# Full contraction rows for the key-value tails, an earlier root for the second half of batch 0, and another order for batch 1's and 2's casts

## The chip, the cores and the metric

The kernel runs on one core of a Trainium2 chip. The metric is the device time of one execution in microseconds (us); lower is better. The kernel before has a median of 335.21 us over three runs (334.85 to 335.27). On the core, TensorE (PE) does the matrix products, VectorE (DVE), ScalarE (ACT) and GpSimd (POOL) the elementwise work and the casts, and SyncE (SP) issues nearly all transfers. PEld is PE's weight load.

## The reference

A linear attention with a normalisation for each head, then a gated feed-forward network (FFN):

```python
# q, k, v: [8, 8, 576, 64] (batch, head, position, head_dim)
kv = np.einsum('bhsd,bhse->bhde', k, v)
out = np.einsum('bhsd,bhde->bhse', q, kv)
rms = np.sqrt(np.mean(out * out, axis=-1, keepdims=True) + 1e-06)
out = out / rms * g_norm
x = out.transpose(0, 2, 1, 3).reshape(8 * 576, 512)
# FFN: w_gate, w_val [512, 1536], w_out [1536, 512]
rms = np.sqrt(np.mean(x * x, axis=-1, keepdims=True) + 1e-06)
xn = x / rms * rms_g
g = xn @ w_gate
result = (g / (1 + np.exp(-g)) * (xn @ w_val)) @ w_out    # [4608, 512], float32
```

## The kernel before, in words

**Tiling.** The 576 positions of a batch are 512 main rows (four tiles of 128) and 64 tail rows. The FFN runs in nine stages of 512 rows: one for the main rows of each batch (n = 0 to 7) and one for the tail rows of all eight (n = 8). A stage has twelve steps `up(j)`: four products with the gate weights into the PSUM tile g_ps, four with the value weights into v_ps, then SiLU on ACT and the multiplication h_sb on DVE. Four steps `down(c)` follow, of twelve products each with w_out into o_ps; ACT copies the result and SP stores it. A step is eight products of 128x512, a `down` twelve.

**Attention.** For each batch, `kv_pair` (L259) multiplies keys and values of two heads into a 128x128 state: for batches 0 and 1 from a packed layout (L264), for batches 2 to 7 (L272) with four products of 128 rows and a fifth of the 64 tail rows, which stand in tile `t == T` of the buffers. There are two key and two value buffers, kbs and vbs, used in turn by even and odd batches. The states go to kv_all (L303, L304). Then come q times state (`o`), squares and sums, an inverse root (`head`, `guess`, `root`), the scaled rows xna (`scale`) and their turn into the layout xnt that the FFN reads.

**Order.** Each engine does its instructions in the order in which the code emits them, and semaphores hold them until their inputs are there. So the order in the code is the schedule. From stage n = 1 on, the lists `steps[u]` hold the work that is emitted behind step u: the attention of the next batch, and casts and loads of the batch after that.

**The start.** Batch 0 is done in two halves of 256 columns: A, then Z. Its root is ACT's Sqrt (L441) and DVE's reciprocal (L444), both in `root_by_table`; then ACT loads its table for SiLU (L718). Weights come in blocks of columns (`load_w`), and `round_w` (L196) casts and scales them to bf16. Block 1 covers steps 2 and 3, block 2 steps 4 to 7, block 3 steps 8 to 11. Half A's columns are used by `up_pair(i, 0)`, half Z's by `up_pair(i, 256)`; between them xna of Z is turned on PE (`x_turn`, L634) and DVE copies it to xnt.

**Between stage 0 and stage 1.** Stage 0's `down` is cut in pieces (`down_part`), and batch 1's attention stands between them: key-value products, the turns of q (L770), the columns `f_cols` and their squares, the sums, F.head and F.root on DVE, F.scale (xna, L448), and `f_x`, which turns xna on PE (L280) and copies it to xnt on ACT or DVE. The PSUM pool att_ps has two banks, so a third tile waits until the first has been read. `round_wo` casts the out weights wo_sb, three blocks of four tiles, `cast_kv` and `cast_q` the keys, values and queries (both through L106 on ACT and L108 on the other engines).

**Loads.** All large loads go through SP in order into a ring of seven staging buffers (`st`); a load waits until the casts of its buffer's old content are done.

Of the kernel before, what the change touches and what calls it, by code (L numbers as in the profile page):

```python
# [20 lines left out]
def kernel(  # L21
# [20 lines left out]
    T = 4  # L42
# [216 lines left out]
    def kv_pair(ps, b, j, first, last):  # L259
        if b < EARLY:  # L260
            for c in range(C):
                for u in range(2):
                    rows = slice(u * D, u * D + D)
                    PE.matmul(  # L264
                        ps[rows, rows], lhsT=pairs_buf(b, "k")[rows, j, c, :], rhs=pairs_buf(b, "v")[rows, j, c, :],
                        start=(first and c == 0), stop=(last and c == C - 1),
                    )
            return
        hs = slice(2 * j, 2 * j + 2)
        for t in range(T + 1):  # L270
            n = TAIL if t == T else 128
            PE.matmul(  # L272
                ps, lhsT=bufs[b]["k"][0:n, t, hs, :], rhs=bufs[b]["v"][0:n, t, hs, :],
                start=(first and t == 0), stop=(last and t == T),
            )

# [430 lines left out]
    for s in range(NS):  # L707
        round_w(1, "g", s, SC)
        round_w(1, "v", s, GP)
# [7 lines left out]
    Z.root_by_table(lambda: None)  # L717
# [3 lines left out]
    xs = [Z.scale(c, oZ[c]) for c in range(2)]  # L721
    halves = [ffn.up_pair(0, 0)]
    ffn.gate_pair(0, 0, halves[0])
    nothing = lambda: None
    turnsZ = (nothing, lambda: x_turn(Z, 0, xs[0], DVE), lambda: x_turn(Z, 1, xs[1], DVE))
    halves.append(ffn.up_pair(1, 0, turnsZ))
# [31 lines left out]
    A1 = None  # L758
# [74 lines left out]
    round_wo_halves(2)  # L833
# [58 lines left out]
    for n in range(1, B + 1):  # L892
# [6 lines left out]
        if n == 1:  # L899
            for i in KV_CASTS:  # L900
                steps[i // 2 % 2] += [lambda i=i: cast_kv(2, "v", i, GP if i == NS else SC if i % 2 else DVE)]
        if n < B:
            a = atts[n + 1]
            late = n == 1
            if not a.tail:
                steps[late] += [lambda a=a: a.kv_products((0, 1))]
                steps[1 + late] += [lambda a=a: a.kv_products((2, 3)), a.kv_copy]
            for c in range(T):
                u = (3, 5, 6, 8)[c] if late else 2 + 2 * c
# [58 lines left out]
```

## Time and profile before

| | |
|---|---|
| median of 3 runs | 335.21 us (334.85 to 335.27) |
| profiled execution | 334.25 us |
| its span on the core | 332.4 us |
| granted TensorE clock | 0.999 |
| loaded and stored | 37.75 MB read, 9.44 MB written |
| stage n = 1 starts (first g_ps of L467) | 59.70 us into the span |

The span is the time from the first to the last instruction that the profiler saw; the execution's time has 1.85 us around it. Times in the rows of a timeline are microseconds from the span's start: start, length, engine, line, operation, output<-inputs, shapes and count, and in brackets the idle time ahead of it with what ended it. Rows of groups give the summed busy time in us and the mean of one in ns. In the table of stretches, the columns are the stretch, its length, the busy time of PE, PEld, DVE, ACT and POOL with counts, the granted PE clock, the busy share of the DMA engines and GB/s.

### The profile page before, as it was taken

The numbers are of one execution on the slowest core, as the hardware profiler recorded it, in microseconds if no ns is written. First come the engines' busy times: TensorE is split into PE (matmuls) and PEld (weight loads), VectorE is DVE, ScalarE is ACT, GpSimd is POOL, SyncE is SP. The second block draws the span as 40 slices with busy tenths as digits, with TensorE's granted clock in tenths as the row PEclk, the third lists the DMA queues.
The fourth block names the chain that finished last, engine by engine and source line by source line (L and its number), as shares of the span: only waits on it lengthen the run. The fifth ranks groups of instructions, "written<-read, shape, count | busy, mean of one in ns | idle before, by whom it ended". The sixth has DMA issues, their size and how long they took to land.

```text
span 332.4 us, 5037 instructions
## 1 busy us (share of the span) xinstructions
PE 318.9 (96%) x1876; PEld 156.5 (47%) x1908; DVE 181.3 (55%) x367; ACT 179.6 (54%) x316; POOL 18.2 (5%) x37
## 2 busy tenths in 40 slices
PE   6889997999999999999999999999999999999994
PEld 3665454554444444444454445444544444444441
DVE  4865658359616771578057905791478156813410
ACT  3577655555765575556655665667465255223321
POOL 1232206100000000000000000000000000000000
PEclk9999999999999999999999999999999999999999
DMA  8999999585279626971697079966300630060014
GB/s 265 346 381 387 374 370 250 179 281 145 47 144 299 177 33 154 299 182 21 153 298 193 16 144 195 297 146 156 95 2 0 153 102 0 3 173 17 0 34 96
DMA packets 73861, 54.87 MB, mean 165 GB/s; under 512 B 42088, under 2 KB 65644, under 8 KB 73836
## 3 DMA queue, kind: packets, MB, share of 16 engines
q1 hardware_dynamic: 73536, 53.95, 58.0%
q10 hardware_dynamic: 300, 0.59, 0.5%
q8 instruction: 15, 0.25, 0.3%
q14 instruction: 10, 0.08, 0.1%
HBM read 37.75 MB, written 9.44 MB: 142 GB/s over the span
## 4 chain that ended last, share of the span: by engine, by line
PE 84%; DMA 5%; DVE 5%; ACT 2%; issue 1%; SPq 1%; DVEq 0%
PE v_ps L467 26%; PE g_ps L467 26%; PE o_ps L504 23%; PE att_ps L272 3%; DMA st<-in_moe_w_gate_dram 3%; DMA st<-in_q_dram 2%; PE att_ps L338 2%; DVE xna L448 1%; SPq L380 1%; DVE xna L373 1%; DMA xnt<-xna 1%; PE v_ps L504 1%; DVE h_sb L473 1%; PE g_ps L484 1%; PE v_ps L484 1%
## 5 line engine op out<-in xcount | busy, mean ns | idle before, releaser
L473 DVE TENSOR_TENSOR h_sb<-silu,v_ps 128x512 bf16<-128x512 bf16 x104 | 71.1, 684 | 113.2 <-PE v_ps L467 71.9
L467 PE MATMUL v_ps<-xnt,wv_sb 128*128 128x512 bf16 x412 | 106.1, 379 | 0.4
L467 PE MATMUL g_ps<-xnt,wg_sb 128*128 128x512 bf16 x399 | 104.5, 379 | 1.2 <-issue 0.5
L472 ACT ACTIVATE silu<-g_ps 128x512 bf16<-128x512 f32 x104 | 62.5, 601 | 68.3 <-PE g_ps L467 62.8
L504 PE MATMUL o_ps<-wo_sb,h_sb 128*128 128x512 bf16 x398 | 89.4, 379 | 0.7 <-issue 0.2
L504 PEld LDWEIGHTS <-h_sb 128*128 128x128 bf16 x432 | 41.2, 98 | 49.8 <-DVE h_sb L473 2.4
L467 PEld LDWEIGHTS <-wv_sb 128*128 128x128 bf16 x416 | 40.7, 98 | 49.1
L467 PEld LDWEIGHTS <-wg_sb 128*128 128x128 bf16 x416 | 38.2, 98 | 41.3 <-issue 1.1
L106 ACT COPY o_sb<-o_ps 128x512 f32<-128x512 f32 x34 | 19.9, 586 | 39.4 <-PE o_ps L504 36.5
L356 DVE TENSOR_REDUCE ssq<-sq 128x16 f32<-128x1024 bf16 x28 | 34.1, 1220 | 1.0
L347 ACT ACTIVATE sq<-att_ps 128x512 bf16<-128x512 f32 x28 | 16.7, 597 | 14.2 <-PE att_ps L338 11.3
L106 ACT CAST vb<-st 128x512 bf16<-128x512 f32 (+2 forms) x35 | 20.5, 630 | 4.8 <-DMA st<-in_v_dram 4.8
L373 DVE TENSOR_TENSOR xna<-outa,s1y 128x512 bf16<-128x512 bf16 x28 | 17.5, 685 | 0.2
L349 ACT CAST outa<-att_ps 128x512 bf16<-128x512 f32 x28 | 16.2, 580 | 0.0
L106 ACT CAST kb<-st 128x512 bf16<-128x512 f32 (+1 forms) x25 | 14.0, 619 | 0.0
L106 ACT CAST qb<-st 128x1024 bf16<-128x1024 f32 (+1 forms) x13 | 12.5, 1009 | 1.0 <-DMA st<-in_q_dram 1.0
L272 PE MATMUL att_ps<-vb,kb 128*128 128x128 bf16 (+1 forms) x120 | 12.4, 222 | 0.0
L355 DVE TENSOR_TENSOR sq<-sq,gsq 128x512 bf16<-128x512 bf16 x28 | 11.7, 418 | 0.0
L272 PEld LDWEIGHTS <-kb 128*128 128x128 bf16 (+1 forms) x120 | 8.6, 97 | 6.1
L338 PEld LDWEIGHTS <-qt 128*128 128x128 bf16 x96 | 7.4, 98 | 5.7
L338 PE MATMUL att_ps<-kv_all,qt 128*128 128x128 bf16 x96 | 9.3, 219 | 0.0
L579 PE MATMUL att_ps<-kv_all 128*128 128x256 bf16 (+1 forms) x34 | 7.5, 352 | 1.2 <-DVE sel L568 1.2
(122 smaller groups left out, 158.5 us busy)
## 6 DMA issues: line engine op xcount, KB each, us to landing
out_dram<-o_sb SPq DMA_DIRECT2D x16, 512.0 KB, 3.1
st<-in_q_dram SPq DMA_DIRECT2D x7, 1024.0 KB, 6.4
st<-in_k_dram SPq DMA_DIRECT2D x6, 1024.0 KB, 9.6
st<-in_v_dram SPq DMA_DIRECT2D x6, 1024.0 KB, 10.9
st<-in_moe_w_out_dram SPq DMA_DIRECT2D x3, 1024.0 KB, 14.8
st<-in_moe_w_gate_dram SPq DMA_DIRECT2D x2, 1024.0 KB, 12.3
st<-in_moe_w_val_dram SPq DMA_DIRECT2D x2, 1024.0 KB, 13.1
st<-in_k_dram SPq DMA_DIRECT2D x4, 288.0 KB, 5.0
```

Source lines behind the costliest of these rows:

```text
L106: engine.copy(out=dst, in_=src)
L272: PE.matmul(ps, lhsT=bufs[b]["k"][0:n, t, hs, :], rhs=bufs[b]["v"][0:n, t, hs, :], start=(first and t == 0), stop=(last and t == T),)
L338: PE.matmul(cols, lhsT=self.qt[:, j, 128 * c : 128 * c + 128], rhs=kv_all[:, self.n, j, :], start=(j == 0), stop=(j == NS - 1),)
L347: SC.activation(out=self.sq[c][:, 0], in_=ps, func=ACT.Square)
L349: SC.copy(out=self.outa[c], in_=ps)
L355: DVE.tensor_tensor(out=sq[:, 1], in0=sq[:, 0], in1=gsq8, op=OP.mult)
L356: DVE.reduce_sum(out=self.ssq[:, c], in_=sq, axis=AX.X)
L373: DVE.tensor_tensor(out=self.xna[c], in0=self.outa[c], in1=self.alpha[:, c, :].to_broadcast([128, H, D]), op=OP.mult)
L467: PE.matmul(ps, lhsT=wt[:, s, j * 128 : (j + 1) * 128], rhs=x[:, s, :], start=(s == 0), stop=(s == NS - 1),)
L472: SC.activation(out=silu, in_=g_ps, func=ACT.Silu)
L473: DVE.tensor_tensor(out=self.h[:, j, :], in0=silu, in1=v_ps, op=OP.mult)
L504: PE.matmul(self.o_ps[c], lhsT=self.h[:, j, c * 128 : (c + 1) * 128], rhs=wo_sb[:, j, :], start=(j == 0), stop=(j == NF - 1),)
```

## The change

The tail product of batches 2 to 7 takes all 128 rows of its tile. The upper 64 rows of the tail tile are set to zero once in each of the four buffers, on POOL (`clear_tail_rows`): in the even pair after half Z has been scaled, in the odd pair after batch 1's products. In the start, Z's root is emitted ahead of the casts of weight block 1, which are shared out over ACT, DVE and POOL; the turns of Z follow the gate products of step pair 1 instead of standing among its value products. For batch 1, v's load moves behind the first out weights, casts of k, v, q, of the out weights and of value weight block 3 change their engines and places, and key-value products and q turns move one `down_part` later. Batch 2's q and k casts leave POOL for ACT and DVE. In stage 1, the key-value products of batch 2 and its first `o` move one step later. From stage 1 on, `guess` is emitted behind step 11 instead of step 10.

```diff
         for t in range(T + 1):
-            n = TAIL if t == T else 128
             PE.matmul(
-                ps, lhsT=bufs[b]["k"][0:n, t, hs, :], rhs=bufs[b]["v"][0:n, t, hs, :],
+                ps, lhsT=bufs[b]["k"][:, t, hs, :], rhs=bufs[b]["v"][:, t, hs, :],
...
+    def clear_tail_rows(i, engine):
+        for t in (kbs[i], vbs[i]):
+            engine.memset(t[TAIL:128, T], 0.0)
...
-    for s in range(NS):
-        round_w(1, "g", s, SC)
-        round_w(1, "v", s, GP)
...
-    Z.root_by_table(lambda: None)
+    Z.root_by_table(lambda: round_w(1, "g", 2, DVE))
+    round_w(1, "g", 0, SC)
+    round_w(1, "g", 3, SC)
+    round_w(1, "g", 1, GP)
     SC.preload_act_table(ACT.Silu)
 
     ffn = Ffn(0)
     xs = [Z.scale(c, oZ[c]) for c in range(2)]
+    for s in range(NS):
+        round_w(1, "v", s, GP if s < 2 else DVE)
+    clear_tail_rows(0, GP)
     halves = [ffn.up_pair(0, 0)]
+    def turnsZ():
+        x_turn(Z, 0, xs[0], DVE)
+        x_turn(Z, 1, xs[1], DVE)
+    halves.append(ffn.up_pair(1, 0, (lambda: None, turnsZ)))
     ffn.gate_pair(0, 0, halves[0])
...
-    for name in ("k", "v"):
-        alloc_kv(1, name)
-        load_kv(1, name, nc.sync)
+    alloc_kv(1, "k")
+    load_kv(1, "k", nc.sync)
     load_wo(0)
+    alloc_kv(1, "v")
+    load_kv(1, "v", nc.sync)
     load_q(1)
...
-    for s in range(NS):
+    for s in (2, 3):
         round_w(3, "v", s, GP)
     for j in range(4, NF):
         ffn.up(j)
         for s in {4: (0, 1), 5: (2,), 6: (3,)}.get(j, ()):
             round_w(3, "g", s, SC)
-        if 5 <= j < 9:
-            cast_kv(1, "k", j - 5, DVE)
+        if j == 6:
+            for s in (0, 1):
+                round_w(3, "v", s, DVE)
         if j >= 8:
-            cast_kv(1, "v", j - 8, SC)
-        if j == 10:
-            round_wo(0, 0, 1, DVE)
-    for i in range(1, 4):
-        round_wo(0, i, 1, GP)
+            cast_kv(1, "k", j - 8, DVE)
+        if j == 7:
+            for i in range(4):
+                round_wo(0, i, 1, GP)
+    for i in range(NS):
+        cast_kv(1, "v", i, DVE if i % 2 else SC)
     for i in range(4):
-        cast_q(1, slice(2 * i, 2 * i + 2), DVE)
+        cast_q(1, slice(2 * i, 2 * i + 2), SC if i == 2 else DVE)
...
-    for c in range(4):
-        down_part(c, 0, 4)
-        if c == 0:
-            att1.kv_products((0, 1, 2, 3))
-            att1.kv_copy()
-        if c in (1, 2):
-            turns.q_turn(c - 1, SC if c == 1 else DVE)
-    round_wo_halves(1)
+    down_part(0, 0, 4)
+    down_part(1, 0, 4)
+    att1.kv_products((0, 1, 2, 3))
+    att1.kv_copy()
+    down_part(2, 0, 4)
+    turns.q_turn(0, SC)
+    turns.q_turn(1, DVE)
+    down_part(3, 0, 4)
+    round_wo(1, 0, 2, DVE)
+    for i in (2, 3):
+        round_wo(1, i, 1, GP)
+    for i in range(4):
+        round_wo(2, i, 1, GP)
+    clear_tail_rows(1, GP)
...
-    round_wo_halves(2)
...
-    f_x(0, xs[0], DVE)
+    f_x(0, xs[0], SC)
     f_x(1, xs[1], SC)
     ffn.down_out(1)
+    alloc_q(2)
+    cast_q(2, slice(0, 4), SC)
     down_part(2, 8, 12)
     f_x(2, xs[2], DVE)
-    f_x(3, xs[3], SC)
+    f_x(3, xs[3], DVE)
...
+    cast_q(2, slice(4, 8), DVE)
...
-    alloc_q(2)
-    for i in range(4):
-        cast_q(2, slice(2 * i, 2 * i + 2), GP)
-    for i in KV_CASTS:
-        cast_kv(2, "k", i, GP)
+    cast_kv(2, "k", 0, DVE)
+    cast_kv(2, "k", 1, DVE)
...
+            steps[0] += [lambda i=i: cast_kv(2, "k", i, DVE) for i in (2, 3)]
+            steps[0] += [lambda i=i: cast_kv(2, "v", i, SC) for i in (0, 1)]
+            steps[1] += [lambda i=i: cast_kv(2, "v", i, SC) for i in (2, 3)]
+            steps[0] += [lambda name=name: cast_kv(2, name, NS, GP) for name in ("k", "v")]
...
-            late = n == 1
+            kv0, os = (2, (4, 5, 7, 8)) if n == 1 else (0, (2, 4, 6, 8))
...
-            steps[10] += [a.head, a.guess]
-            steps[11] += [a.root]
+            steps[10] += [a.head]
+            steps[11] += [a.guess, a.root]
```

Three places in the engines' orders. The first is ACT in the start, from the squares of Z to the first SiLU (sqt are squares, Zs is Z's root, wg_sb the cast of gate weights). Before:

```order
L630 ACTIVATE sqt<-g_ps 128x2x256
L630 ACTIVATE sqt<-v_ps 128x2x256
L201 ACTIVATE wg_sb<-st,rowscale 128x256 x4
L441 ACTIVATE Zs<-Zz 128x16
L718 ACT_TABLE_LOAD
L494 ACTIVATE silu<-g_ps 128x512 x2
```

And in the changed kernel:

```order
L634 ACTIVATE sqt<-g_ps 128x2x256
L634 ACTIVATE sqt<-v_ps 128x2x256
L445 ACTIVATE Zs<-Zz 128x16
L201 ACTIVATE wg_sb<-st,rowscale 128x256 x2
L722 ACT_TABLE_LOAD
L498 ACTIVATE silu<-g_ps 128x512 x2
```

The root stands ahead of the weight casts, and two of the four casts have gone to other engines.

The second is POOL from the first weights on (qb, kb, vb are casts of queries, keys and values). Before:

```order
L203 TENSOR_SCALAR wg_sb<-st,rowscale 128x256 x4
L203 TENSOR_SCALAR wv_sb<-st,rowscale 128x256 x8
L203 TENSOR_SCALAR wv_sb<-st,rowscale 128x512 x4
L108 CAST wo_sb<-st 128x512 x3
L108 CAST qb<-st 128x4x128 x4
L108 CAST kb_119<-st 128x4x128 x4
L108 CAST kb_119<-st 64x512
L108 CAST vb_121<-st 64x512
```

And in the changed kernel:

```order
L203 TENSOR_SCALAR wv_sb<-st,rowscale 128x256 x2
L279 MEMSET kb_119 64x512
L279 MEMSET vb_121 64x512
L203 TENSOR_SCALAR wv_sb<-st,rowscale 128x512 x2
L108 CAST wo_sb<-st 128x512 x10
L279 MEMSET kb_120 64x512
L279 MEMSET vb_122 64x512
L108 CAST kb_119<-st 64x512
L108 CAST vb_121<-st 64x512
```

POOL has ten casts of out weights and four clears, and of batch 2 only the tails.

The third is ACT from the rows of batch 1's attention (outa) to the first SiLU of stage 1. Before:

```order
L106 CAST outa<-att_ps 128x512 x4
L106 COPY o_sb<-o_ps 128x512
L106 COPY xnt<-att_ps 128x4x128
L106 COPY o_sb<-o_ps 128x512
L106 COPY xnt<-att_ps 128x4x128
L106 COPY o_sb<-g_ps 128x512
L106 COPY o_sb<-v_ps 128x512
```

And in the changed kernel:

```order
L106 CAST outa<-att_ps 128x512 x4
L106 COPY o_sb<-o_ps 128x512
L106 COPY xnt<-att_ps 128x4x128 x2
L106 COPY o_sb<-o_ps 128x512
L106 CAST qb<-st 128x4x256
L106 COPY o_sb<-g_ps 128x512
L106 COPY o_sb<-v_ps 128x512
```

ACT copies the first and second turned block, DVE now the third and fourth, and half of batch 2's queries stands ahead of ACT's last two output copies.

More of the change, by code (lines that the diff above doesn't have):

```diff
@@ L754 @@
     broadcast_gsq()
-    A1 = None
     alloc_q(1)
@@ L899 @@
         if n == 1:
-            for i in KV_CASTS:
-                steps[i // 2 % 2] += [lambda i=i: cast_kv(2, "v", i, GP if i == NS else SC if i % 2 else DVE)]
+            steps[0] += [lambda i=i: cast_kv(2, "k", i, DVE) for i in (2, 3)]
+            steps[0] += [lambda i=i: cast_kv(2, "v", i, SC) for i in (0, 1)]
+            steps[1] += [lambda i=i: cast_kv(2, "v", i, SC) for i in (2, 3)]
+            steps[0] += [lambda name=name: cast_kv(2, name, NS, GP) for name in ("k", "v")]
         if n < B:
             a = atts[n + 1]
-            late = n == 1
+            kv0, os = (2, (4, 5, 7, 8)) if n == 1 else (0, (2, 4, 6, 8))
             if not a.tail:
[L906 to L909, printed above, removed]
+                steps[kv0] += [lambda a=a: a.kv_products((0, 1))]
+                steps[kv0 + 1] += [lambda a=a: a.kv_products((2, 3)), a.kv_copy]
+            for c, u in enumerate(os):
                 steps[u].append(lambda a=a, c=c: a.o(c))
                 steps[u + 1].append(lambda a=a, c=c: a.sums(c))
-            steps[10] += [a.head, a.guess]
-            steps[11] += [a.root]
+            steps[10] += [a.head]
+            steps[11] += [a.guess, a.root]
             for c in range(T):
```

3 lines of the change are left out of this document (removed).

## The prediction

> **What bounds the kernel now.** I read the page's busy shares and its chain of work first, then the busy time in stretches of 10 us, then the timeline where TensorE (PE) is not full.
>
> ```profile
> PE 318.9 (96%) x1876; PEld 156.5 (47%) x1908; DVE 181.3 (55%) x367; ACT 179.6 (54%) x316; POOL 18.2 (5%) x37
> ...
> PE 84%; DMA 5%; DVE 5%; ACT 2%; issue 1%; SPq 1%; DVEq 0%
> ```
>
> ```profile
> 20.00:30.00 10.00, 8.66 (x67) 5.96 (x68) 7.73 (x15) 7.95 (x14) 1.77 (x4) 1.00 1.05 386
> 50.00:60.00 10.00, 8.01 (x72) 4.57 (x75) 7.80 (x17) 5.73 (x11) 7.18 (x10) 1.00 0.94 258
> ```
>
> PE sets the pace: 96% busy, and 84% of the chain that ends last. So a term counts if it shortens PE's own work, or if it closes one of PE's holes and nothing else holds PE right behind. After the start there are two holes: PE has 8.66 of 10 us from 20 on and 8.01 from 50 on (the first number after the stretch's length). The clock is granted in full (1.00), and the DMA engines are saturated from 20 to 30 (1.05, 386 GB/s).
>
> **The padded tails.** Rows of the timeline: eight 128x128 products of full rows and what starts after them, then one group of ten products of keys and values, two of them the 64-row tails; and the groups by form.
>
> ```profile
> 44.19 0.61 PE L770 MATMUL att_ps<-identity,qb 128*128 128x128 bf16 x8
> 44.63 1.03 PE L504 MATMUL g_ps<-wo_sb,h_sb 128*128 128x512 bf16 x4
> ...
> 63.15 1.03 PE L272 MATMUL att_ps<-vb,kb 128*128 128x128 bf16 x10
> 64.12 1.04 PE L467 MATMUL g_ps<-xnt,wg_sb 128*128 128x512 bf16 x4
> ```
>
> ```profile
> L272 PE MATMUL att_ps<-vb,kb 128*128 128x128 bf16 x96 | 9.4, 220 | 0.0
> L272 PE MATMUL att_ps<-vb,kb 64*128 64x128 bf16 x24 | 5.4, 227 | 0.0
> ```
>
> Matmuls overlap, so I go from start to start. Eight full ones take 44.63 - 44.19 = 0.44 us, 0.055 each; ten would take 0.55. The ten with two tails take 64.12 - 63.15 = 0.97, so a tail costs (0.97 - 0.55) / 2 = 0.21 more than a full product, a little less unrounded. There are 24 tails (six batches, four pairs of heads): 24 x 0.205 = **4.9 us**. All of it lies where PE runs without a hole, in the first steps of six stages, and the steps after it keep their distances to each other. With 128 rows the tail becomes one more product of the form around it. The bounds are 0 (the pause comes from something else) and 4.9; I take 4.9, since no other row than the tail differs within the group.
>
> The Trainium skill says otherwise in "TensorE: Matmul & The Clock Gate", section "Why this matters for your kernels": a single matmul with few contraction rows takes the same time as a full one. By that rule the padding is worth nothing. The means above (227 against 220 ns) agree with it for one matmul by itself, the starts do not. "TensorEngine Tiling (Array Packing)", section "Key Properties", states that a change of tiling mode drains the engine, which would be the pause on both sides of a tail.
>
> The four clears are memsets of 64x512 on POOL. The nearest row:
>
> ```profile
> masks.py:197 POOL MEMSET identity<- 128x128 bf16 x1 | 0.2, 205 | 0.3 <-POOLq L952 0.3
> ```
>
> That is 0.2 us for a quarter of the elements per partition, so 0.2 to 0.8 us each. The first two stand on POOL where it would wait for weights; the other two count below.
>
> **The second half's root.** The rows of that stage:
>
> ```profile
> 18.23 0.17 DVE L229 SCALAR_TENSOR_TENSOR Zz<-Zm,att_ps 128x16 f32<-128x16 f32 x1
> 18.38 1.71 ACT L201 ACTIVATE wg_sb<-st,rowscale 128x256 bf16<-128x256 f32 x4 [1.68 <-DMA st<-in_moe_w_gate_dram]
> ...
> 19.99 0.20 ACT L441 ACTIVATE Zs<-Zz 128x16 f32<-128x16 f32 x1
> ...
> 20.58 1.29 DVE L448 TENSOR_TENSOR xna<-o_ps,Zal 128x512 bf16<-128x512 f32 x2
> ...
> 23.54 1.05 PE L484 MATMUL g_ps<-xnt,wg_sb 128*128 128x256 bf16 x8 [0.72 <-DVE xnt L108]
> ...
> 25.29 0.88 DVE L203 TENSOR_SCALAR wv_sb<-st,rowscale 128x512 bf16<-128x512 f32 x2 [1.21 <-DMA st<-in_moe_w_val_dram]
> ...
> 27.92 0.48 DVE L203 TENSOR_SCALAR wv_sb<-st,rowscale 128x512 bf16<-128x512 f32 x1
> ...
> 28.15 1.03 PE L467 MATMUL v_ps<-xnt,wv_sb 128*128 128x512 bf16 x4
> ```
>
> The root Zs needs only Zz (18.40), but stands behind four weight casts until 19.99. Ahead of them it runs at about 18.45, so xna starts at about 19.05 instead of 20.58. The two added casts of value weights on DVE (0.5 us by half the L203 row, up to twice that beside POOL) come before the xnt copies, which then end at 21.8 to 22.3, and PE starts the second half of its columns 1.3 to 1.6 us before 23.54. But that lead does not last. DVE casts the next block of value weights from 25.29, where it waited 1.21 us for their transfer, and transfers do not get faster (1.05). From there DVE has the same work as before; only a small wait (under 0.2 us) ahead of the last cast goes, so that cast ends at about 28.2 instead of 28.40. PE needs it for the fourth product of L467, before at 28.15 + 3 x 0.215 = 28.80. So PE can lead by at most 28.8 - 28.2 = 0.6 there. The bounds are 0 and 1.6; I take 0.6.
>
> **Batch 1 between the two FFN stages.** The rows of that stage:
>
> ```profile
> 36.80 0.45 DVE L108 CAST kb<-st 128x576 bf16<-128x576 f32 x1
> ...
> 39.59 1.92 POOL L108 CAST wo_sb<-st 128x512 bf16<-128x512 f32 x3 [5.99 <-DMA st<-in_moe_w_out_dram]
> 39.60 4.39 SPq L133 DMA_DIRECT2D st<-in_k_dram  x1
> ...
> 44.04 3.66 SPq L137 DMA_DIRECT2D st<-in_k_dram  x1
> ...
> 47.49 1.02 PE L504 MATMUL o_ps<-wo_sb,h_sb 128*128 128x512 bf16 x4
> ...
> 48.02 0.69 DVE L108 CAST wo_sb<-st 128x1024 bf16<-128x1024 f32 x1 [0.58 <-DMA st<-in_moe_w_out_dram]
> ...
> 50.34 0.38 PE L422 MATMUL att_ps<-kv_all,qt 128*128 128x128 bf16 x4
> 50.52 0.36 DVE L223 RECIPROCAL Fr<-att_ps 128x32 f32<-128x32 f32 x1 [1.80 <-PE att_ps L414]
> ...
> 51.15 2.30 POOL L108 CAST qb<-st 128x512 bf16<-128x512 f32 x4 [9.64 <-DMA st<-in_q_dram]
> ...
> 52.40 0.53 DVE L239 SCALAR_TENSOR_TENSOR F0c<-F0a,Fz 128x32 f32<-128x32 f32 x1
> ...
> 52.96 1.89 PE L504 MATMUL o_ps<-wo_sb,h_sb 128*128 128x512 bf16 x8
> 53.52 0.19 DVE L237 TENSOR_TENSOR F1a<-F0y 128x32 f32<-128x32 f32 x1
> ...
> 54.27 3.74 DVE L448 TENSOR_TENSOR xna<-outa,F1y 128x512 bf16<-128x512 bf16 x4
> 54.76 4.28 POOL L108 CAST kb<-st 128x512 bf16<-128x512 f32 x5 [1.30 <-DMA st<-in_k_dram]
> ...
> 58.39 0.61 PE L280 MATMUL att_ps<-identity,xna 128*128 128x128 bf16 x8 [1.10 <-DVE xnt L108]
> ...
> 59.36 0.61 POOL L108 CAST vb<-st 64x512 bf16<-64x512 f32 x1 [0.33 <-DMA st<-in_v_dram]
> ...
> 59.70 1.03 PE L467 MATMUL g_ps<-xnt,wg_sb 128*128 128x512 bf16 x4
> ...
> 60.56 1.03 PE L467 MATMUL v_ps<-xnt,wv_sb 128*128 128x512 bf16 x4
> ```
>
> ```profile
> L373 DVE TENSOR_TENSOR xna<-outa,s1y 128x512 bf16<-128x512 bf16 x28 | 17.5, 685 | 0.2
> L106 ACT COPY o_sb<-o_ps 128x512 f32<-128x512 f32 x34 | 19.9, 586 | 39.4 <-PE o_ps L504 36.5
> ```
>
> How much PE loses: from 52.96 to 59.70 it starts 16 products of 512 columns, at (60.56 - 59.70) / 4 = 0.215, and 16 transposes at 0.055: 3.45 + 0.9 = 4.35 us of work in 6.74. So 2.39 us are lost, all behind xna and xnt.
>
> Why xna is late: the same kind of DVE instruction takes 0.53 us while POOL casts (F0c) and 0.19 when POOL has stopped (F1a); three of them are hit, 1.0 us. The four xna take 3.74 us beside POOL's kb casts, where 685 ns each is usual. In the changed kernel POOL has none of those q and k casts. It has six casts of out weights, the last four from the landing at 48.02; at 1.92 / 3 = 0.64 each they end at 50.6, and the clears at 51.0 to 52.2.
>
> What is late next: down_part(0, 4, 6), at 47.49 before, follows a cast of out weights that DVE does after its qt copy, and ACT's squares come behind; I give 0.15 of the 0.6 away there (an estimate, the length of a wait ahead of it, not of a new instruction). So the sums end at about 49.9 instead of 50.34, and Fr starts at 50.05. Fr to xna took 54.27 - 50.52 = 3.75; less 1.0 that is 2.75, so xna starts at 52.8 and the first is done at 53.5, the second at 54.1. PE comes to f_x(0) at 49.9 + (52.96 + 1.72 - 50.34) = 54.25: no wait. ACT copies the first two turned blocks (0.6 each, from 54.6) by 55.8, so f_x(3) gets its bank some 0.15 late; DVE, done with xna at 55.4, copies the other two by 56.8, where PE arrives. Of 2.39, **2.24 go**, and the lead of **0.45** stays. If the clears hit the three DVE instructions after all, xna comes 1.0 later and PE loses about 0.6. The Trainium skill ("SBUF — State Buffer", "Who interferes with whom") has two-input DVE instructions contend with POOL only when POOL reads SBUF; by it the clears cost nothing here, which no run so far shows.
>
> What I cost at nothing, with its cover. **Batch 2's q casts** go to ACT (two halves of the size in the o_sb row, so about 1.0) and DVE: silu(0) is then some 0.8 late, and its bank is next needed a whole step (eight products, 1.72) later. **The k casts** go to DVE between the first steps, and products of batch 2 move one step later, behind them. **v of batch 1** lands where the first out weights landed, at 39.6; its casts, two each on ACT and DVE, have the eight products of down_part(0) and down_part(1) (1.7 us) before the first pair needs one, and more before the last. **k2's load** takes the buffer of batch 1's k, whose last cast (36.80 + 0.45) comes three steps later, 37.25 + 3 x 1.72 - 0.6 = 41.8. SP came to that load at 39.60, so it is held for 2.2 us, and on SP the k tail, v2 and v's tail stand behind it. A k tail of 128 KB kept SP for 3.66 us, so the queue was full and has that to give; if not, v's tail lands at 61.6 instead of 59.36, POOL's cast (0.61) ends at 62.2, and PE, there after three steps (57.0 + 3 x 1.72 = 62.2), waits up to 0.3.
>
> **guess behind h(11)** in the later stages is the last of these:
>
> ```profile
> 153.13 0.68 DVE L473 TENSOR_TENSOR h_sb<-silu,v_ps 128x512 bf16<-128x512 bf16 x1
> ```
>
> No wait stands in brackets: DVE is the one that is behind, so the same instructions in another order end when they did, and xna starts when it did.
>
> The sum: 334.25 (the profiled execution, span 332.4 and 1.85 around it) - 4.9 - 0.45 - 2.24 = **326.66**. The median of the runs shown, 335.21, lies 0.96 above the profiled execution, so on its scale the forecast is **327.6 us**.
>
> **Rivals.**
> *The tails were not slow because of their rows.* Then 4.9 stays: 331.56, or 332.5 on the median's scale. For it speaks only the mean of 227 ns; 0.97 against 0.55 in the same group speaks against. 4%.
> *PE still waits for xna or xnt*, because the clears or the last out weights still run on POOL, or ACT's copies come late: 0.6 to 2.2 of the 2.39 stay, so 328.2 to 329.8. The clears' length is unknown, so 11%.
> *The early lead holds*, because the value weights land sooner: 1.0 more, 326.6. 1.05 in the DMA column speaks against. 5%.
> *Slower: POOL becomes the bound.* down_part(0, 8, 12) needs the four casts from 48.02, its last product at about 53.1. A cast took 0.64, at worst a mean of 4.28 / 5 = 0.86 beside busy DVE: 51.5, in time. Above (53.1 - 48.0) / 4 = 1.3 us PE waits, and above (53.1 + 7.6 - 48.0) / 4 = 3.2 us the kernel is slower than before. Nothing in the rows is near. 3%, a third of it within 0.2% of before.
>
> **How the numbers follow.** The forecast has 77%, the rivals 23%. The range takes in the early lead and most of a remaining wait: 326.3 to 330.0. Within 0.2% (0.67 us, about what a measurement of this kernel can tell from no change) I put 1%, slower 2%, faster 97%: only the last rival ends on those sides.
>
> **What would show it.** Right: ten products of keys and values from start to start in about 0.56; Zs ahead of the weight casts and PE waiting near 27 to 28 for DVE's L203; F0a to F0y at 0.19 and xna at 0.69; no PE hole over 0.3 between 54 and 57; the first g_ps of batch 1's stage at about 57.0. Wrong: a tail still set off by 0.15 on either side; POOL busy into F0a; a wait of PE on vb or kb near 62; holes between later stages that were not there.

## The result and the profile after

The changed kernel takes **327.12 us** (median of four runs, 326.96 to 328.01) against 335.08 us for the kernel before in four runs beside it: a ratio of 0.9768, 95% interval 0.9749 to 0.9787, so 2.3% faster. The forecast was 327.6 us, with a range of 326.3 to 330.0. The profiled execution took 327.04 us, with a span of 325.2 and the clock granted in full (1.000).

The page of the changed kernel, its busy shares and its chain of work:

```profile
PE 315.5 (97%) x1908; PEld 156.4 (48%) x1908; DVE 181.7 (56%) x374; ACT 178.3 (55%) x314; POOL 16.8 (5%) x37
...
PE 90%; DMA 5%; SPq 1%; DVE 1%; POOL 1%; issue 0%; ACT 0%
```

PE's share of the chain of work that ends last has grown from 84% to 90%. The busy time by stretches says where (stretch, length, then PE's busy time):

```profile
20.00:30.00 10.00, 9.24 (x73) 6.40 (x71) 7.23 (x15) 7.70 (x13) 1.98 (x4) 1.00 1.05 387
50.00:60.00 10.00, 10.00 (x76) 5.50 (x73) 7.92 (x22) 8.07 (x15) 2.51 (x5) 1.00 1.03 288
120.00:130.00 10.00, 9.19 (x58) 4.62 (x57) 1.80 (x3) 5.52 (x11) 0.00 (x0) 1.00 0.62 151
```

The hole from 50 on is gone (10.00 of 10, before 8.01) and the one from 20 on is smaller. But from 120 on there is a hole (9.19) that the forecast doesn't have. I take the places one by one, in timelines of the changed kernel.

**Keys and values**, in stage n = 1:

```profile
62.12 0.72 PE L271 MATMUL att_ps<-vb,kb 128*128 128x128 bf16 x10
62.68 0.38 PE L471 MATMUL g_ps<-xnt,wg_sb 128*128 128x512 bf16 x1
```

Ten products take 62.68 - 62.12 = 0.56 us from start to start. Before it was 0.97.

**The start**, from Z's root to step 5 of stage 0:

```profile
18.54 0.21 ACT L445 ACTIVATE Zs<-Zz 128x16 f32<-128x16 f32 x1 [1.74 <-DVE Zz L229]
18.66 0.89 ACT L201 ACTIVATE wg_sb<-st,rowscale 128x256 bf16<-128x256 f32 x2
...
22.07 1.04 PE L488 MATMUL g_ps<-xnt,wg_sb 128*128 128x256 bf16 x8
...
25.47 0.88 DVE L203 TENSOR_SCALAR wv_sb<-st,rowscale 128x512 bf16<-128x512 f32 x2 [2.35 <-DMA st<-in_moe_w_val_dram]
...
27.86 0.48 DVE L203 TENSOR_SCALAR wv_sb<-st,rowscale 128x512 bf16<-128x512 f32 x1
...
28.40 0.39 PE L471 MATMUL v_ps<-xnt,wv_sb 128*128 128x512 bf16 x1 [0.59 <-DVE wv_sb L203]
28.63 0.81 PE L471 MATMUL g_ps<-xnt,wg_sb 128*128 128x512 bf16 x3
```

The root now stands ahead of the weight casts, at 18.54 instead of 19.99, and half Z's columns start at 22.07 instead of 23.54. This lead of 1.47 is cut down at the fourth value product of L471, which waits for DVE's last cast of value weights (27.86 + 0.48 = 28.34). It starts at 28.40; before, it started at 28.80. So 0.40 us of lead are left.

**Between stages 0 and 1**, batch 1's root, scaling and turns:

```profile
50.44 0.52 POOL L279 MEMSET kb<- 64x512 bf16 x1
50.54 0.19 DVE L225 TENSOR_TENSOR Ft<-Fr,att_ps 128x32 f32<-128x32 f32 x1
...
50.90 0.52 POOL L279 MEMSET vb<- 64x512 bf16 x1
...
51.72 0.19 DVE L239 SCALAR_TENSOR_TENSOR F0c<-F0a,Fz 128x32 f32<-128x32 f32 x1
...
52.58 1.89 PE L508 MATMUL o_ps<-wo_sb,h_sb 128*128 128x512 bf16 x8
...
52.92 2.50 DVE L452 TENSOR_TENSOR xna<-outa,F1y 128x512 bf16<-128x512 bf16 x4
...
54.31 0.61 PE L284 MATMUL att_ps<-identity,xna 128*128 128x128 bf16 x8
...
56.94 1.03 PE L471 MATMUL g_ps<-xnt,wg_sb 128*128 128x512 bf16 x4
```

F0c takes 0.19 instead of 0.53, the four xna 2.50 instead of 3.74. No row of PE between 52.58 and 56.94 has a wait in brackets: 4.36 us for the 4.35 us of work that stand there. Stage n = 1 starts at 56.94 instead of 59.70, 2.76 us earlier.

**The new hole** stands ahead of stage n = 3, at the end of stage n = 2 (SPq is SyncE's queue):

```profile
116.53 6.26 SPq L384 DMA_TRANSPOSE xnt<-xna  x4
...
124.17 1.02 PE L471 MATMUL g_ps<-xnt,wg_sb 128*128 128x512 bf16 x4 [0.81 <-DMA xnt<-xna]
```

In stage n = 3 the four transposes take 5.16 us in all; here they take 6.26, and PE waits 0.81 us for xnt. In the changed kernel's DMA queues, between 116.0 and 118.5 us, there is one transfer that isn't a transpose:

```profile
q8 instruction: 1, 0.02, 3.2%
```

It is a load of program code, 16 KB, one of 15 in the whole execution. PE issues 1908 products and 1908 weight loads; 3816 / 15 is 254 of them for each load, so these loads look like PE's program. This load comes at 117.2, in the first transpose, which takes 2.34 us; the same transpose takes 1.23 in the run below that shifts the loads.

Lengths of stages, from the first g_ps of one to the first g_ps of the next, in the profiled executions, and the median times (all runs of the next section included):

| kernel | time, us | n = 1 starts | n = 1 | n = 2 | n = 3 to 6 | n = 7 |
|---|---|---|---|---|---|---|
| before | 335.08 | 59.70 | 33.95 | 34.28 | 33.95 | 33.12 |
| changed | 327.12 | 56.94 | 33.16 | 34.06 | 33.09 | 32.99 |
| 64-row tails | 332.16 | 56.97 | 33.98 | 34.44 | 33.93 | 33.58 |
| padding alone | 329.86 | 59.95 | 33.12 | 33.37 | 33.12 | 33.70 |
| 64-row tails together | 330.04 | 56.75 | 33.57 | 34.30 | 33.51 | 34.06 |
| root behind casts | 326.99 | 57.03 | 33.17 | 33.69 | 33.09 | 33.31 |
| q and k casts on POOL | 329.88 | 59.31 | 33.17 | 33.40 | 33.09 | 33.05 |
| copies as before | 327.95 | 57.83 | 33.15 | 33.29 | 33.09 | 34.07 |
| value weights shared | 327.33 | 56.56 | 33.16 | 34.32 | 33.09 | 33.47 |
| code loads shifted | 326.15 | 57.25 | 33.17 | 33.09 | 33.09 | 32.88 |
| both of these | 326.05 | 57.19 | 33.16 | 33.09 | 33.09 | 32.88 |
| and full rows for epsrow and gsq | 325.76 | 56.68 | 33.15 | 33.09 | 33.09 | 32.88 |

Within a kernel, stages 3 to 6 repeat to 0.02 us. What scatters from kernel to kernel is the start, and stages 2 and 7. The times come from four comparisons: the first two rows, the next four, the next four and the last two. In them the kernel before took 335.08, 334.9, 335.2 and 334.8 us, so a few tenths of a us between rows of different comparisons mean little.

### The profile page after: what moved, and what is told of

It is laid out like the page before. It is cut to its first block, busy times and chain, and to the rows that moved or that the text cites. A ratio compares the mean times of both kernels' runs of the same rounds, so it can differ in the third digit from the quotient of the medians.

```text
span 325.2 us, 5068 instructions
## 1 busy us (share of the span) xinstructions
PE 315.5 (97%) x1908; PEld 156.4 (48%) x1908; DVE 181.7 (56%) x374; ACT 178.3 (55%) x314; POOL 16.8 (5%) x37
## 4 chain that ended last, share of the span: by engine, by line
PE 90%; DMA 5%; SPq 1%; DVE 1%; POOL 1%; issue 0%; ACT 0%
PE g_ps L471 28%; PE v_ps L471 27%; PE o_ps L508 26%; DMA st<-in_moe_w_val_dram 3%; PE att_ps L271 2%; DMA st<-in_q_dram 2%; PE att_ps L342 2%; PE v_ps L488 1%; SPq L384 1%; PE g_ps L508 1%; PE g_ps L488 1%; PE v_ps L508 1%; DMA xnt<-xna 1%; POOL wv_sb L203 1%; PE att_ps L337 0%; PE att_ps L284 0%
## 5 line engine op out<-in xcount | busy, mean ns | idle before, releaser
L471 PE MATMUL v_ps<-xnt,wv_sb 128*128 128x512 bf16 x416 | 106.9, 379 | 0.8 <-DVE wv_sb L203 0.6
L471 PE MATMUL g_ps<-xnt,wg_sb 128*128 128x512 bf16 x416 | 106.8, 379 | 0.8 <-DMA xnt<-xna 0.8
L508 PEld LDWEIGHTS <-h_sb 128*128 128x128 bf16 x432 | 41.9, 98 | 49.3 <-issue 0.3
L471 PEld LDWEIGHTS <-wv_sb 128*128 128x128 bf16 x416 | 40.7, 98 | 50.3 <-DVE wv_sb L203 1.2
L471 PEld LDWEIGHTS <-wg_sb 128*128 128x128 bf16 x416 | 38.5, 98 | 41.2 <-issue 2.2
L106 ACT CAST qb<-st 128x1024 bf16<-128x1024 f32 (+1 forms) x15 | 14.2, 987 | 1.9 <-DMA st<-in_q_dram 1.9
L271 PEld LDWEIGHTS <-kb 128*128 128x128 bf16 x120 | 7.7, 98 | 2.8
L271 PE MATMUL att_ps<-vb,kb 128*128 128x128 bf16 x120 | 8.7, 219 | 0.0
```

The lines of the kernel that those rows point to most:

```text
L106: engine.copy(out=dst, in_=src)
L271: PE.matmul(ps, lhsT=bufs[b]["k"][:, t, hs, :], rhs=bufs[b]["v"][:, t, hs, :], start=(first and t == 0), stop=(last and t == T),)
L471: PE.matmul(ps, lhsT=wt[:, s, j * 128 : (j + 1) * 128], rhs=x[:, s, :], start=(s == 0), stop=(s == NS - 1),)
L508: PE.matmul(self.o_ps[c], lhsT=self.h[:, j, c * 128 : (c + 1) * 128], rhs=wo_sb[:, j, :], start=(j == 0), stop=(j == NF - 1),)
```

## The experiments

All are edits of the changed kernel, but for the second one.

### Tails with 64 rows

```diff
+            n = TAIL if t == T else 128
             PE.matmul(
-                ps, lhsT=bufs[b]["k"][:, t, hs, :], rhs=bufs[b]["v"][:, t, hs, :],
+                ps, lhsT=bufs[b]["k"][0:n, t, hs, :], rhs=bufs[b]["v"][0:n, t, hs, :],
```

> The changed kernel with the tail products of 64 rows again (the clears stay). Theory (a change of the row count makes PE pause on both sides of a tail): ten products of a group from start to start 0.97 us instead of 0.56, and 12 groups x 0.41 to 0.44 = 4.9 to 5.2 us more than the changed kernel's 327.1, so 332.0 to 332.3. Rival (a tail of 64 rows costs no more than one of 128, and the gain came from elsewhere): 327.1.

332.16 us (331.62 to 333.86, five runs), a ratio of 0.9921 (0.9894 to 0.9947) to the kernel before, and 5.04 us above the changed kernel's median. In its timeline the same group of ten, and what starts after it:

```profile
62.15 1.03 PE L272 MATMUL att_ps<-vb,kb 128*128 128x128 bf16 x10
63.11 1.04 PE L472 MATMUL g_ps<-xnt,wg_sb 128*128 128x512 bf16 x4
```

0.96 again, and stages of 33.93 instead of 33.09. The start of stage n = 1 has not moved (56.97). So the rows of the tails alone are worth 0.84 in each of six stages, 5.0 us.

### The padding alone, in the kernel before

```diff
-            n = TAIL if t == T else 128
             PE.matmul(
-                ps, lhsT=bufs[b]["k"][0:n, t, hs, :], rhs=bufs[b]["v"][0:n, t, hs, :],
+                ps, lhsT=bufs[b]["k"][:, t, hs, :], rhs=bufs[b]["v"][:, t, hs, :],
...
     xs = [Z.scale(c, oZ[c]) for c in range(2)]
+    clear_tail_rows(0, GP)
...
     round_wo_halves(1)
+    clear_tail_rows(1, GP)
```

> The kernel before with the full-row tails and the clears alone. Theory: 335.1 - 4.9 to 5.2 = 329.9 to 330.2, each stage from n = 1 on shorter by 0.82 to 0.87 us (33.95 before), and the holes between 54 and 60 us as before. Rival (other work takes the place of the pauses): less than half of it, 332.6 or more.

329.86 us (329.54 to 329.99), 0.9845 (0.9825 to 0.9864): 5.0 us below the 334.9 us of the kernel before in the same comparison. The stages take 33.12, and stage n = 1 starts at 59.95 (59.70 before), with no gain there. The other parts of the change are worth the remaining 2.7 us. Stages of the changed kernel are still 0.03 shorter (33.09), and the edit left for that is `guess` behind step 11: 0.03 in each of six stages, 0.2 us. I had costed it at nothing; it was not tried alone.

### 64-row tails side by side

The two tails of a group stand behind its eight full products, instead of one in the middle and one at the end.

```diff
+            for ts in ((range(T + 1),) if self.n < EARLY else (range(T), (T,))):
                 for j in js:
-                    kv_pair(self.kv_ps[:, j, :], self.n, j, j == 0, j == NS - 1)
+                    kv_pair(self.kv_ps[:, j, :], self.n, j, j == 0, j == NS - 1, ts)
```

> The changed kernel with 64-row tails, the two tails of a group put together behind its eight full products. Theory (the pause belongs to the change of row count): one change in and one out for two tails, so half of e1's cost, 12 x 0.2 = 2.5 us over 327.1: 329.6. Rival (each 64-row product is slow by itself): as e1, 332.0 to 332.3.

330.04 us (329.42 to 330.37), 0.985 (0.9827 to 0.9872). That is 0.4 above the 329.6 expected; stage n = 7 takes 34.06 here instead of 32.99, with a code load in its transposes. In its timeline:

```profile
61.93 0.82 PE L272 MATMUL att_ps<-vb,kb 128*128 128x128 bf16 x10
62.69 1.04 PE L473 MATMUL g_ps<-xnt,wg_sb 128*128 128x512 bf16 x4
```

The group takes 0.76: 0.20 over full rows, half of the 0.40 of two separate tails, with the same products and the same rows. So the price isn't one of a 64-row product but of a change from 128 rows to 64 and back, 0.20 us. The Trainium skill, "TensorEngine Tiling (Array Packing)", section "Key Properties", says that a change of tiling mode drains the engine; the halving agrees with that. The Trainium skill's rule in "TensorE: Matmul & The Clock Gate", section "Why this matters for your kernels", that a single matmul with few rows takes the time of a full one, agrees with the length of the product itself (227 ns against 220 in the kernel before), not with the starts around it.

### Z's root behind the weight casts again

```diff
     squares(Z, 1, banksZ[1])
+    for s in range(NS):
+        round_w(1, "g", s, SC)
+        round_w(1, "v", s, GP)
...
-    Z.root_by_table(lambda: round_w(1, "g", 2, DVE))
-    round_w(1, "g", 0, SC)
-    round_w(1, "g", 3, SC)
-    round_w(1, "g", 1, GP)
+    Z.root_by_table(lambda: None)
...
-    for s in range(NS):
-        round_w(1, "v", s, GP if s < 2 else DVE)
```

With the root, the casts of block 1 go back to ACT and POOL alone.

> The changed kernel with Z's root behind the weight casts on ACT and POOL, as before the change; all else stays. Theory (the early lead ends at the landing of the second weight block's values): PE's wait for wv_sb near 28 goes, and the stage n = 1 starts 0.4 to 0.6 us later, 327.6. Rival (the whole lead reached the end): 1.5 us more, 328.6.

326.99 us (326.76 to 327.18), 0.976 (0.9737 to 0.9783): no difference from the changed kernel, and stage n = 1 starts at 57.03, 0.09 later. PE's wait for wv_sb is gone, as expected, but the 0.4 to 0.6 us were missed. The timeline shows why:

```profile
20.23 0.20 ACT L445 ACTIVATE Zs<-Zz 128x16 f32<-128x16 f32 x1
...
22.03 0.41 DVE L108 COPY xnt<-att_ps 128x512 bf16<-128x512 bf16 x1
...
22.94 1.29 DVE L499 TENSOR_TENSOR h_sb<-silu,v_ps 128x512 bf16<-128x512 bf16 x2
...
23.27 1.04 PE L488 MATMUL g_ps<-xnt,wg_sb 128*128 128x256 bf16 x8
...
27.87 1.03 PE L471 MATMUL v_ps<-xnt,wv_sb 128*128 128x512 bf16 x4
...
28.73 0.59 PE L471 MATMUL g_ps<-xnt,wg_sb 128*128 128x512 bf16 x2
```

In the kernel before, DVE had these in the other order:

```profile
22.14 0.69 DVE L495 TENSOR_TENSOR h_sb<-silu,v_ps 128x512 bf16<-128x512 bf16 x1 [0.26 <-ACT silu L494]
...
22.74 0.75 DVE L108 COPY xnt<-att_ps 128x512 bf16<-128x512 bf16 x2
```

The root is late, as in the kernel before, and yet half Z's columns start 0.27 before 23.54. Two things are left that can do it, and they belong together: the two turns of Z stand behind the gate products, and the first h_sb (`gate_pair`) has moved behind them, so that DVE copies xnt ahead of it. From there nothing holds PE: the value products of L471 run through without a wait, and the next step starts at 28.73 (before 29.01, changed 28.63). So this order alone brings PE to within 0.1 us of the changed kernel, whose PE waits there for DVE's value-weight casts, and most of what the early root adds is lost at that wall. The turns and the h_sb were not tried apart.

### Batch 2's query and key casts back on POOL

```diff
-    alloc_q(2)
-    cast_q(2, slice(0, 4), SC)
...
-    cast_q(2, slice(4, 8), DVE)
...
-    cast_kv(2, "k", 0, DVE)
-    cast_kv(2, "k", 1, DVE)
+    alloc_q(2)
+    for i in range(4):
+        cast_q(2, slice(2 * i, 2 * i + 2), GP)
+    for i in range(NS):
+        cast_kv(2, "k", i, GP)
```

(The two key casts in stage 1 go as well.)

> The changed kernel with batch 2's q casts and four main k casts back on POOL, as before. Theory (POOL's casts slow the root and xna, and that made PE's hole): F0a to F0y 0.53 us instead of 0.19 again, the four xna about 3.7 us instead of 2.50, and stage n = 1 starts 1.5 to 2.2 us later than 56.94: 328.6 to 329.3. Rival (the hole closed because ACT and DVE share out the copies to xnt otherwise): under 0.5 us, 327.6 at most.

329.88 us (329.15 to 330.13), 0.9839 (0.9822 to 0.9857), and stage n = 1 starts at 59.31, 2.37 later:

```profile
51.53 2.30 POOL L108 CAST qb<-st 128x512 bf16<-128x512 f32 x4
51.53 0.65 DVE L237 TENSOR_TENSOR F0a<-Fyi 128x32 f32<-128x32 f32 x1
...
54.42 3.74 DVE L452 TENSOR_TENSOR xna<-outa,F1y 128x512 bf16<-128x512 bf16 x4
...
55.17 0.40 PE L284 MATMUL att_ps<-identity,xna 128*128 128x128 bf16 x4 [0.67 <-DVE xna L452]
```

The slow F0a, the slow xna and PE's wait for them are all back, and the loss is a little above the 1.5 to 2.2 expected. All else of the new order is in place, so with POOL's casts nearly the whole hole is there again.

### The turned blocks' copies as before

```diff
-    f_x(0, xs[0], SC)
+    f_x(0, xs[0], DVE)
...
-    f_x(3, xs[3], DVE)
+    f_x(3, xs[3], SC)
```

> The changed kernel with the four copies to xnt shared out as before (DVE, ACT, DVE, ACT). Theory (POOL's casts were the main cause): a small part, 0.3 to 0.6 us, because the first copy waits behind all xna on DVE and the last behind the q cast on ACT: 327.4 to 327.7. Rival (the copies were the main cause): 1.5 us or more.

327.95 us (327.44 to 328.24), 0.9778 (0.9762 to 0.9794). Stage n = 1 starts at 57.83, 0.89 later than in the changed kernel:

```profile
53.25 2.50 DVE L452 TENSOR_TENSOR xna<-outa,F1y 128x512 bf16<-128x512 bf16 x4
...
57.18 0.60 ACT L106 COPY xnt<-att_ps 128x512 bf16<-128x512 bf16 x1
...
57.83 1.02 PE L471 MATMUL g_ps<-xnt,wg_sb 128*128 128x512 bf16 x4 [0.23 <-ACT xnt L106]
```

0.33 of that is older than this stage: xna itself starts 0.33 later, in the scatter of the start. From xna to the first g_ps it is 57.83 - 53.25 = 4.58 instead of 4.02, so the copies' engines are worth 0.56. ACT copies the last block behind its half of batch 2's queries, and PE waits for it. So the hole closes by both edits: without the one nothing of the gain is left, without the other 0.56 of it goes.

### Value weights shared with ACT and POOL

The wall of the start: the third and fourth cast of block 2's value weights leave DVE.

```diff
-        round_w(2, "v", 2 + i, DVE)
+        round_w(2, "v", 2 + i, SC if i else GP)
```

> The changed kernel, of the second weight block's value casts the third on POOL and the fourth on ACT instead of DVE. Theory (that DVE's last cast is the wall at which the early lead ends): PE's wait for wv_sb near 28 goes from 0.6 to under 0.1, and stage n = 1 starts 0.5 to 0.75 us earlier than 56.94: 326.4 to 326.6. Rival (another landing right behind holds PE): under 0.2 us earlier, 327.0.

327.33 us (326.98 to 328.0), 0.9763 (0.9745 to 0.9781), no gain that shows in the time. In the timeline:

```profile
25.36 1.32 DVE L203 TENSOR_SCALAR wv_sb<-st,rowscale 128x512 bf16<-128x512 f32 x2 [1.82 <-DMA st<-in_moe_w_val_dram]
25.50 0.91 POOL L203 TENSOR_SCALAR wv_sb<-st,rowscale 128x512 bf16<-128x512 f32 x1 [3.34 <-DMA st<-in_moe_w_val_dram]
...
28.19 1.03 PE L471 MATMUL g_ps<-xnt,wg_sb 128*128 128x512 bf16 x4
```

The wall is gone and step 5 starts 0.44 earlier than in the changed kernel, less than expected. Beside POOL's cast DVE's two take 1.32 instead of 0.88. Stage n = 1 starts 0.38 earlier. Stages 2 and 7 take that back: 34.32 and 33.47 (34.06 and 32.99 in the changed kernel), with code loads at 117.0 and 283.5 in their transposes.

### Code loads shifted

Eleven products of two columns more among the warm-up products at the start, 22 instructions of PE, so that the loads of its program fall elsewhere.

```diff
     warm(warm_ps, 9)
+    warm(warm_ps, 11, 2)
```

> The changed kernel with eleven more products of two columns each at the start, 22 more instructions in PE's program, so that each load of 16 KB of PE's code comes about 2 us earlier from then on. They compute nothing that is used. Theory (stage n = 2 ends 0.9 us late because such a load, at 117.2, falls into the transposes of xna that SP issues from 116.5 on): the first transpose of that stage is issued in 1.2 us instead of 2.3, the stage takes 33.1 us instead of 34.06, and the time is 326.2. Rival (DVE or the loads of the next batch hold the transposes): stage n = 2 stays at 34.0, 327.1.

**326.15 us** (325.98 to 326.45), 0.9726 (0.9709 to 0.9744), 0.97 below the changed kernel's median, by products whose results nobody reads, and though stage n = 1 starts 0.31 later. Its timeline at the place of the new hole:

```profile
116.85 5.16 SPq L384 DMA_TRANSPOSE xnt<-xna  x4
...
123.51 1.03 PE L471 MATMUL g_ps<-xnt,wg_sb 128*128 128x512 bf16 x4
```

The code load comes at 115.7 instead of 117.2, ahead of the transposes, and the one in stage 7 at 280.9 instead of 283.6. The transposes take 5.16, PE waits for nothing, and every stage from 2 to 6 takes 33.09. The new hole was this collision.

### Both edits, and full rows for epsrow and gsq

The shared value weights and the shifted loads in one kernel:

> The changed kernel with both edits that have been timed one at a time: the third and fourth value-weight cast of block 2 on POOL and ACT (alone: stage n = 1 starts 0.38 us earlier, but stages n = 2 and n = 7 are held by code loads), and 11 narrow products more at the start (alone: every stage 33.09, 326.15). If the cast's gain was real and only eaten by code loads that meet the transposes, the two add: stage n = 1 starts near 56.9 (57.25 less 0.38), no stage above 33.2, and the time is 325.8 (325.5 to 326.1). If the gain was a matter of chance in the start, the time is 326.15 as with the narrow products alone. If the shifted loads meet transposes again after the start has moved by 0.4, one stage is longer by 0.5 to 1.2 and the time is 326.5 to 327.2.

326.05 us (325.88 to 326.35), 0.9737 (0.9722 to 0.9752); the 0.10 below the shifted loads alone lies between two comparisons and says nothing. Step 5 starts at 28.53, 0.42 before the 28.95 of the kernel with shifted loads, so the cast's gain in the start is real; but stage n = 1 starts only 0.06 earlier. The timeline of the combined kernel shows where it goes:

```profile
45.59 1.17 POOL L108 CAST wo_sb<-st 128x512 bf16<-128x512 f32 x2 [6.23 <-DMA st<-in_moe_w_out_dram]
...
46.27 1.04 DVE L108 CAST wo_sb<-st 128x1024 bf16<-128x1024 f32 x1
...
47.37 0.81 PE L508 MATMUL o_ps<-wo_sb,h_sb 128*128 128x512 bf16 x3 [0.35 <-DVE wo_sb L108]
```

PE is early, but POOL's cast of out weights begins when their load lands, and that has hardly moved (45.59; with the shifted loads alone 45.65). DVE's cast now starts at 46.27 instead of 46.69, falls into POOL's and takes 1.04 (0.68 there), and PE waits 0.35. This is the next wall, and it is again a landing. None of the three expected outcomes is quite this one.

The last kernel takes 128 rows for two more kinds of 64-row products, those of epsrow and of gsq. It isn't every other one, as the expectation has it: the packed 64x64 products of batches 0 and 1 (L264) stay as they are.

```diff
-    ones = consts.tile([64, 128], BF16, name="ones")
-    epsrow = consts.tile([64, H], BF16, name="epsrow")
+    ones = consts.tile([128, 128], BF16, name="ones")
+    epsrow = consts.tile([128, H], BF16, name="epsrow")
...
-    DVE.memset(epsrow[0:32], eps_hi / 32)
-    DVE.memset(epsrow[32:64], eps_lo / 32)
+    DVE.memset(epsrow[0:64], eps_hi / 64)
+    DVE.memset(epsrow[64:128], eps_lo / 64)
...
-            ps[:, 0:D], lhsT=gsq[0:D, :].to_broadcast([D, 128]), rhs=identity[0:D, 0:D], start=True, stop=True
+            ps[:, 0:D], lhsT=gsq.to_broadcast([128, 128]), rhs=identity[:, 0:D], start=True, stop=True
```

> The kernel of the run before, and every other 64-row product of the start takes 128 rows too: the eight products of epsrow with ones (the constant is spread over 128 rows instead of 64) and the one that spreads gsq over the partitions (its other rows meet zeros of the identity). If the pause of 0.10 us on each side belongs to every change of the row count, each of these gives back up to 0.2: F's products stand between full-row ones on the way to stage n = 1, so that n = 1 starts 0.2 to 0.6 earlier, and the time is 325.2 to 325.6. If these pauses lie in waits of PE for DVE and ACT, which end no earlier, nothing changes: within 0.1 of the run before.

**325.76 us** (325.52 to 325.96), 0.9728 (0.9713 to 0.9743), 0.3 below the run before, in the same comparison, and between the two outcomes expected. The products of epsrow with 64 rows, in the kernel before this one:

```profile
49.09 0.59 PE L508 MATMUL v_ps<-wo_sb,h_sb 128*128 128x512 bf16 x2
49.62 0.25 PE L415 MATMUL att_ps<-epsrow,ones 64*128 64x8 bf16 x4
...
50.22 0.38 PE L426 MATMUL att_ps<-kv_all,qt 128*128 128x128 bf16 x4
```

and with 128:

```profile
48.70 0.59 PE L508 MATMUL v_ps<-wo_sb,h_sb 128*128 128x512 bf16 x2
49.13 0.24 PE L415 MATMUL att_ps<-epsrow,ones 128*128 128x8 bf16 x4
...
49.64 0.38 PE L426 MATMUL att_ps<-kv_all,qt 128*128 128x128 bf16 x4
```

From the first row to the last it is 0.94 instead of 1.13: one change of rows and back, 0.19, the price that the tails had. From v_ps to epsrow it is 0.43 instead of 0.53, and from there to the last row 0.51 instead of 0.60, so the pause lies about half on each side. The single product of gsq gives back 0.20 as well: from the eight value products ahead of it to the first of step 4 behind it, it is 0.90 (25.05 to 25.95) instead of 1.10 (25.39 to 26.49). But PE then waits 0.32 for DVE's h_sb. Stage n = 1 starts 0.51 earlier (56.68). Of this 0.39 stands ahead of the rows shown; step 5 already starts 0.37 earlier (28.16), and that start scatters by 0.3 between kernels alike there (28.63 and 28.95 in the changed kernel and the one with shifted loads). And 0.07 is lost behind these rows. So for the time 0.19 is shown, and the rest isn't.

## Why the prediction was right, point by point

In the profiled executions 7.21 us went (334.25 to 327.04), where the sum had 7.59, so on this scale the forecast was 326.66 and the time came out 0.38 above it. On the median's scale it came out 0.5 below 327.6. The 0.96 added between the scales did not recur: the changed kernel's median lies 0.08 above its profiled execution, while the profiled execution of the kernel before was quicker than any of its four timed runs (334.85 on; in the later comparisons they go from 334.16 to 335.82). The medians differ by 7.96; where the other 0.75 lies, in runs of the kernel before that left no trace, stays open. So the miss of 0.5 is made of 0.38 too much from the terms and 0.88 the other way from the scale; that they offset each other is luck. What follows is the 7.21:

| term | predicted | measured | from |
|---|---|---|---|
| tails | -4.9 | -5.0 | stages of 33.95 against 33.12 with the padding alone, six times |
| early lead | -0.45 | -0.37 | the product behind the sums (L422, now L426) starts at 49.97 instead of 50.34 |
| hole between stages 0 and 1 | -2.24 | -2.39 | 2.76 - 0.37 |
| guess behind h(11) | 0 | -0.2 | 33.12 against 33.09, six stages |
| collisions with code loads | not seen | +0.5 | stage n = 2: 0.97 over 33.09, before 0.33 over 33.95; stage n = 7: 32.99, before 33.12 |
| rest | 0 | +0.2 | stage n = 1 (0.07), what follows the start of stage n = 8 (0.1) |

**Tails.** Mechanism and size were right, and two runs from both sides give it: 5.0 us added by taking the rows away, 5.0 gained by the padding alone. The rival that the tails are slow for another reason is out.

**Early lead.** The size was nearly right, 0.37 for 0.45, by two errors that offset each other: the lead at the wall was 0.40 instead of 0.6, and of the 0.15 that was to be lost behind it only 0.03 went. The wall, DVE's last value-weight cast, stood close to where the forecast had it (28.34 for 28.2), and PE waited there. The cause was given wrongly: the text credits the root, but the turns of Z, put together ahead of the first h_sb, reach within 0.1 us of the same start of step 5 alone. The root is worth 0.09 in the profiled executions, less than the scatter of the start, and nothing in the medians. The text on the change names the new place of the turns, and the prediction gave it no term. A wall that caps two edits hides which of them reaches it.

**The hole.** Putting POOL's casts back costs 2.37, as much as the hole's 2.39, and putting the copies back costs 0.56 of it. The forecast kept 0.15 for a late bank of f_x(3); nothing of it showed. The clears stood beside Ft, Fm, Fz and Fyi: two of 0.52 end at 51.42, before F0a. Ft, Fm and Fz keep their 0.19. Fyi takes 0.26, where the same operation of later stages takes 0.17, and PE doesn't wait for that. The Trainium skill ("SBUF — State Buffer", "Who interferes with whom") has clears spare even DVE instructions with two SBUF inputs. The changed kernel can't show that, since the instructions beside its clears read at most one operand from SBUF, but two of its variants do: F0c starts within a clear with the 64-row tails together (51.58, the clear runs from 51.22 to 51.78) and with the value weights shared (51.45, from 51.09 to 51.65), and takes 0.19 in both. That casts hit such instructions is shown as well, 0.52 for F0c in the run with POOL's casts against 0.19.

**Costed at nothing.** Batch 2's casts on ACT and DVE and the held load of k cost at most the 0.07 by which stage n = 1 is longer than the later ones: the first products of batch 2's keys and values start at 62.12 without a wait. Batch 1's later v casts lie between step 5 and the sums, where the lead shrinks by 0.03.

**What the forecast missed** is listed there as a sign against it, holes between later stages: stage n = 2 lost 0.97 to what looks like a load of PE's own program. It offset what the terms gave more than forecast, so the total came out closer than the understanding was. The kernel before had such a loss too: its stage n = 2 took 34.28 where the others took 33.95, and the prediction didn't ask why.

## What to carry to other kernels

Look at products in a stream from start to start, not by their mean: 227 ns against 220 hid a pause of 0.20 us around each 64-row product, and zeros in the unused rows, written once, bought 5 us. When an edit gives PE a lead, find the next fixed landing or cast that it runs into, and credit the lead to the edit that first reaches it; here the second edit added at most 0.09, and a third one's 0.42 shrank to 0.06 at the next wall. And before a last microsecond is hunted in the schedule, see whether long DMA transposes coincide with code loads: here 22 instructions more at the start moved them so that no transpose of xnt was lengthened.

## What the runs showed of the hardware

- **A change between 64 and 128 contraction rows costs PE about 0.10 us each way.** Four measurements of one change and back agree: 0.20 for one tail among full products, 0.20 for two side by side, 0.19 for four products of epsrow (0.10 ahead of them, 0.09 behind), 0.20 for one of gsq.
- **A 16 KB load of program code holds up a DMA transpose that it falls into:** 2.34 us instead of 1.23 at 117.2, and PE waits 0.81 for the last of them. The Trainium skill, "Advanced Engine Details and Errata", section "ISA Cache", gives 256 instructions for a 16 KB line; 254 of PE's instructions for each load agree. In the traces of the two kernels and of the first seven experiments, 18 transposes of xnt took 1.5 to 2.6 us, one in stage 2 and one in stage 7 of each, and each has such a load within 0.9 us of its start; the three kernels with shifted loads have neither. In those kernels loads still fall into transposes of q (2.35 us at 259.0 with the loads shifted alone), but PE doesn't wait for these. A load that ends just inside a transpose leaves it as it is: in the combined kernel one ends 0.15 us after the start of the transpose at 282.0, which takes 1.19. By which path the load delays the transpose was not tried.
- **POOL's casts slow DVE's casts too, not only the products of two operands on which the forecast rested:** DVE's value-weight casts go from 0.44 to 0.66 each, its cast of out weights from 0.68 to 1.04.
- **POOL's clears spare DVE's products of two operands, but not Fyi,** which reads one: beside the clears it takes 0.26 in the changed kernel and 0.60 in the last one, against 0.17 for the same operation of later stages. In the last kernel xna then starts 3.29 us behind the product that follows the sums instead of 2.95.
